# Hashed attention and a feed-forward layer on one core: the first units rearranged, and later heads' maxima half a head closer to their use

## The chip, the cores and the metric

The kernel runs on 1 core of one Trainium2 chip. Times are device microseconds (us). Lower is better. The time before is the median of 3 runs.

## What is computed

```python
# q, k, v: (4, 8, 768, 64); proj: (64, 6); w_in: (512, 2048); w_out: (2048, 512); all float32
q_bucket = sum((q @ proj > 0) * 2**[0..5]);  k_bucket = the same of k
mask = q_bucket[:, None] == k_bucket[None, :]
scores = where(mask, q @ k.T / 8, -1e9)
attn = exp(scores - max(scores)); attn /= attn.sum() + 1e-9
x = (attn @ v), heads side by side: 3072 tokens x 512
h = x @ w_in
g = h if h >= 1, 0 if h <= -1, else (h + 1)**2 / 4
out = g @ w_out
```

There are 32 heads (batch times heads) of 768 queries and keys, taken as 16 pairs of heads.

## The kernel before, in words

**Precision.** Every product is made of three matmuls on float32 values split in a high part and a remainder: high by high, high by low, low by high. Casts make the high parts, subtractions (`sub`, L38, so all of them have line L39 in the profile) the remainders.

**Units.** The attention part works through 384 units. Unit g is head g // 12, one half of its 384 + 384 queries (g % 12 // 6) and one block of 128 keys (g % 6). In this document "unit 6" of a head is the first unit of its second half. A unit makes its scores with two matmuls (L350, L351; `s`), whose operands hold high and low parts and, in eight extra rows, the six hash bits, scaled by 2**36, and the negative row maximum, so that the matmul itself masks and subtracts. ACT takes the exponential twice, once to the rounded high part `ph` (L359) and once in full (L364; `pf` where POOL does the subtraction, otherwise in place). The remainder `pl` is `pf - ph`: on POOL for key blocks 0 and 3, on DVE for the others (`lo_unit`). Four units later (LAG = 4) three matmuls (L383 to L385) add the unit's product with v to an output bank `o`: bank 0 (`obank[0]`) for the first half of the queries, bank 1 for the second. After the last block of a half ACT copies the bank out (L391).

**The maxima.** Before a head's scores can be made, its row maxima of masked products of high parts must be known. For each of its 6 blocks of queries two matmuls (L310, `max_mm`) write to the only `smax` buffer, and DVE reduces it (L314, `max_red`) one unit later. After six such steps, three further steps bring the result into a row: `max_clamp` (L321 and L323, two small operations, on DVE for heads 2 and 3 and on POOL from head 4 on), `max_tr` (L328, a transpose on PE into a bank of `o`) and `max_put` (L333: ACT copies the transpose to `te`, and two DMAs on SP's queue carry it to the row of the operand and to memory).

**Pairs ahead.** While pair p runs, pair p + 2 is prepared: POOL casts the raw q and k (L150) and takes their remainders (L155) in units 0 to 3 of the first (even) head, one cast and one subtraction in each; SP moves parts between partitions (`move`, L161); `bits_mm` (L204, four matmuls) makes the hash bits in unit 7 in bank 1 and in unit 11 in bank 0, each followed by ACT's negative copy (L210) and DVE's comparison (L215); `bits_scale` (L273, POOL) and `bits_put` (L282, four DMAs) store them. The v of pair p + 1 is cast on ACT in unit 6 (L289) and its remainders are taken on POOL in units 7 and 9.

**Order.** Nothing is reordered by a scheduler: each engine's queue holds its instructions in the order in which the program emits them, and an instruction that waits holds up all behind it. In each unit g the loop (L578 to L599) emits: the scores and exponentials of unit g; the reduction of the maxima begun in the unit before; the remainder of unit g - 1; the product with v of unit g - 4; two maxima matmuls if due; and at last the list `tasks[g]`, in the order in which `at` filled it. The splitting of the feed-forward weights, entered first (L1128 and L1140), thus precedes the attention's own tasks of the same unit: in unit 7 of even heads from head 4 on ACT squares a weight tile (L69), in unit 5 it casts one (L87).

**The schedule of the maxima.** Head 0's first three query blocks are reduced by `max_first` ahead of unit 0; a table `early` (L574 to L577) says in which units the maxima of heads 0 to 4 go, up to unit 36; from there on, head h + 2 gets its six steps in units 0, 2, 4, 6, 8, 10 of head h. In terms of the following head, h + 1, the clamp is in its unit 0, the transpose (into bank 1) in its unit 4, the copy in its unit 5 (L543 to L546). Head h + 2 needs the row at its own unit 0.

**The opening.** Pair 0 has no pair ahead of it to hide behind. Lines L436 to L493 load it, make its bits with a faster path (`prep_first`, `place_first`, `first_mm`, `first_cmp`, `first_scale`), reduce its first maxima and write the first half of the row of head 0 by a matmul with the identity (`row_half`, L263). Matmuls on zeros (`keep_busy`, L402) fill pauses. Pair 1's raw data and pair 0's v are loaded in this order (L464, L465), and both heads' remaining steps, with the preparation of pair 1 in quarters (`quarter`), stand in the tasks of units 0 to 15 (L504 to L537).

After the attention comes the feed-forward part (two passes over the weights, PE busy throughout), which the change does not touch.

The statement that sets the place of clamp, transpose and copy:

```python
gc, gt = ((NU + 8, NU + 8), (2 * NU + 4, 2 * NU + 6))[hd] if hd < 2 else (g + NU, g + NU + 4)
at(gc, max_clamp, hd + 2, nc.gpsimd if hd > 1 else nc.vector)
at(gt, max_tr, hd + 2, 1)
at(gt + (hd > 1), max_put, hd + 2)
```

## Time and profile before

| What | Value |
|---|---|
| Median of the runs | 985.98 us (985.34 to 986.76, 3 runs) |
| Profiled execution, its own time | 986.29 us |
| Its span, first to last instruction | 984.5 us |
| Mean granted clock of TensorE | 0.996 |
| HBM | 142 GB/s over the span |

The engines are PE (TensorE's matmuls), PEld (its weight loads, which overlap the matmuls), DVE (VectorE), ACT (ScalarE), POOL (GpSimd) and SP, whose queue issues nearly all DMAs. L12 is line 12 of the kernel. A row of the order of time reads: start, length, engine, line, operation, output <- inputs, shape, number of instructions in it, and in brackets how long the engine had stood idle before it and what ended that. A list of waits reads: who waited, for whom, us in total, times, longest. A row of busy times by stretch gives, for each stretch, its length, each engine's busy time with its number of instructions, the granted clock as a share of full speed, the DMA engines' share and GB/s. The lengths of matmuls overlap: back to back, a matmul of 384 columns is issued every 0.175 us or so, though each row shows 0.34.

### The profile page before, as it was taken

The numbers are of one execution on the slowest core, as the hardware profiler recorded it, in microseconds if no ns is written. First come the engines' busy times: TensorE is split into PE (matmuls) and PEld (weight loads), VectorE is DVE, ScalarE is ACT, GpSimd is POOL, SyncE is SP. The second block draws the span as 40 slices with busy tenths as digits, with TensorE's granted clock in tenths as the row PEclk, the third lists the DMA queues.
The fourth block names the chain that finished last, engine by engine and source line by source line (L and its number), as shares of the span: only waits on it lengthen the run. The fifth ranks groups of instructions, "written<-read, shape, count | busy, mean of one in ns | idle before, by whom it ended". The sixth has DMA issues, their size and how long they took to land.

```text
span 984.5 us, 15564 instructions
## 1 busy us (share of the span) xinstructions
PE 968.2 (98%) x5047; PEld 891.9 (91%) x5047; DVE 799.5 (81%) x1359; ACT 679.3 (69%) x1483; POOL 342.1 (35%) x411
## 2 busy tenths in 40 slices
PE   7999999999999999999999999999999999999998
PEld 5789999999999999999999998888988888988896
DVE  8789999999999999988798887887876777655554
ACT  6779888998999888988655556555564545554444
POOL 7666777778877777766100000000000000000000
PEclk8999999999999999999999999999999999999999
DMA  6654667766656667554496478977449554454431
GB/s 174 177 154 101 174 179 191 199 173 168 177 140 180 173 187 191 136 146 124 127 286 217 118 245 271 299 239 210 118 151 245 147 185 116 130 168 118 115 93 64
DMA packets 94712, 167.55 MB, mean 170 GB/s; under 512 B 13940, under 2 KB 51432, under 8 KB 94632
## 3 DMA queue, kind: packets, MB, share of 16 engines
q1 hardware_dynamic: 94408, 166.56, 59.3%
q8 instruction: 40, 0.66, 0.3%
q14 instruction: 40, 0.33, 0.1%
q10 hardware_dynamic: 224, 0.00, 0.0%
HBM read 106.13 MB, written 33.87 MB: 142 GB/s over the span
## 4 chain that ended last, share of the span: by engine, by line
PE 90%; DVE 5%; ACT 2%; DMA 1%; issue 1%; SPq 0%; DVEq 0%
PE y L791 27%; PE h L1023 18%; PE smax L310 7%; PE h L928 7%; PE o L385 6%; PE s L351 6%; PE o L384 6%; PE o L383 6%; PE s L350 6%; PE o L204 2%; DVE nm L314 2%; DMA vraw<-in_v_dram 1%; DVE pl L39 1%; DMA t<-te 1%; ACT ph L359 0%
## 5 line engine op out<-in xcount | busy, mean ns | idle before, releaser
L359 ACT ACTIVATE ph<-s 128x384 fp32r<-128x384 f32 x380 | 188.1, 495 | 47.5 <-PE s L351 41.8
L314 DVE TENSOR_REDUCE nm<-smax 128x1 f32<-128x768 f32 x189 | 178.9, 947 | 16.2 <-PE smax L310 14.5
L39 POOL TENSOR_TENSOR pl<-pf,ph 128x384 fp32r<-128x384 f32 x128 | 139.0, 1089 | 90.4 <-ACT pf L364 90.1
L756 DVE SCALAR_TENSOR_TENSOR t<-t 128x384 f32<-128x384 f32 x128 | 71.3, 557 | 101.7 <-ACT z L751 101.5
L39 DVE TENSOR_TENSOR pl<-s,ph 128x384 fp32r<-128x384 f32 x256 | 135.5, 544 | 10.2 <-ACT s L364 9.4
L350 PE MATMUL s<-t 128*128 128x384 f32 x384 | 132.6, 345 | 0.0
L385 PE MATMUL o<-pl,va 128*128 128x386 f32 x384 | 130.6, 340 | 0.4 <-DVE pl L39 0.4
L384 PE MATMUL o<-ph,vb 128*128 128x386 f32 x384 | 130.6, 340 | 0.0
L351 PE MATMUL s<-t 128*128 128x384 f32 x384 | 130.3, 339 | 0.2 <-DMA t<-te 0.2
L383 PE MATMUL o<-ph,va 128*128 128x386 f32 x384 | 130.2, 339 | 0.1
L364 ACT ACTIVATE s<-s 128x384 f32<-128x384 f32 x252 | 124.9, 496 | 0.0
L791 PE MATMUL y<-t,ghi 128*128 128x512 f32 x384 | 124.6, 395 | 0.0
L310 PE MATMUL smax<-t 128*128 128x384 f32 x378 | 104.0, 356 | 6.6 <-DVE nm L314 6.1
L750 ACT ACTIVATE t<-h,mh 128x384 f32<-128x384 f32 x56 | 32.6, 581 | 84.4 <-PE h L928 44.3
L310 PEld LDWEIGHTS smax<-t 128*128 128x128 f32 x378 | 65.5, 191 | 23.5 <-DVE nm L314 23.0
L761 ACT CAST ghi<-z 128x384 fp32r<-128x384 f32 x129 | 65.1, 505 | 30.1 <-DVE z L757 26.3
L751 ACT ACTIVATE z<-t,m 128x384 f32<-128x384 f32 x128 | 79.0, 617 | 4.2
L1023 PE MATMUL h<-wbig,t 128*128 128x384 f32 x399 | 81.4, 336 | 0.0
L791 PEld LDWEIGHTS y<-t,ghi 128*128 128x128 f32 x384 | 71.3, 188 | 11.1 <-ACT ghi L761 0.3
L1023 PEld LDWEIGHTS h<-wbig,t 128*128 128x128 f32 x399 | 71.6, 188 | 5.3
L791 PE MATMUL y<-t,glo 128*128 128x512 f32 x192 | 76.0, 396 | 0.0
L791 PE MATMUL y<-woh,glo 128*128 128x512 f32 x192 | 75.7, 394 | 0.2
(181 smaller groups left out, 2092.0 us busy)
## 6 DMA issues: line engine op xcount, KB each, us to landing
t<-wc SPq DMA_DIRECT2D x92, 256.0 KB
t<-t SPq DMA_DIRECT2D x60, 384.0 KB
wraw<-wc SPq DMA_DIRECT2D x76, 256.0 KB
raw<-in_qk_dram SPq DMA_DIRECT2D x15, 768.0 KB
wraw<-in_w_in_dram SPq DMA_DIRECT2D x16, 512.0 KB
wraw<-in_w_out_dram SPq DMA_DIRECT2D x16, 512.0 KB
t<-ed SPq DMA_DIRECT2D x36, 192.0 KB
xd<-xs SPq DMA_DIRECT2D x32, 192.5 KB
```

The costliest lines, as they stand in the source:

```text
L39: eng.tensor_tensor(out=out, in0=a, in1=b, op=ALU.subtract)
L310: nc.tensor.matmul(out=smax[hd][:, hf, 0:HS], lhsT=t2[:, 0, h, i * P:(i + 1) * P], rhs=t2[:, 1, h, hf * HS:(hf + 1) * HS], start=True, sto ...
L314: nc.vector.tensor_reduce(out=nmp(hd)[:, i:i + 1], in_=smax[hd][:, :, 0:HS], axis=AX.XY, op=ALU.max, negate=True)
L350: nc.tensor.matmul(out=ps[:, 0:HS], lhsT=t1[:, 1, h, ks], rhs=t1[:, 0, h, sl], start=True, stop=False)
L351: nc.tensor.matmul(out=ps[:, 0:HS], lhsT=t2[:, 1, h, ks], rhs=t2[:, 0, h, sl], start=False, stop=True)
L359: nc.scalar.activation(out=ph[:, 0:HS], in_=ps[:, 0:HS], func=AF.Exp, scale=SCALE)
L364: nc.scalar.activation(out=pf, in_=ps[:, 0:HS], func=AF.Exp, scale=SCALE)
L383: nc.tensor.matmul(out=o, lhsT=wa, rhs=ph, start=(jj == 0), stop=False)
L384: nc.tensor.matmul(out=o, lhsT=wb, rhs=ph, start=False, stop=False)
L385: nc.tensor.matmul(out=o, lhsT=wa, rhs=pl, start=False, stop=(jj == NJ - 1))
L791: nc.tensor.matmul(out=ys[c][m], lhsT=g_[:, m * P:(m + 1) * P], rhs=w, start=(first and k == 0), stop=(last and k == 2))
L1023: nc.tensor.matmul(out=ps, lhsT=w[:, cs], rhs=x, start=(n == 0 and s not in (2, 3, 6)), stop=(n == 5), skip_group_check=True)
```

## The change

- **v first.** Pair 0's v is loaded ahead of pair 1's raw data, and the latter in two halves of the columns.
- **More on POOL at the start.** The projection's high parts, the cast of pair 0's v, head 1's two scalings (`first_scale`) and the `row_flags` go from ACT and DVE to POOL; the rows of ones and part of the remainders come earlier on POOL's queue.
- **First units.** Head 0's fourth block of maxima goes ahead of unit 0. Head 1's row is written in two halves (units 9 and 14) and not at once (unit 10). Pair 1's quarters go to units 1, 4, 5 and 6, its bits to units 8 and 10, its stores to unit 12; pair 2's casts begin in unit 16 (before: 9), its bits stand in units 20 and 24 (before: 13 and 17). One `move` takes its source from another copy of the same data.
- **Maxima half a head later, for all heads.** The table `early` ends at unit 30; from there on head h + 2 gets its maxima in units 6, 8, 10 of head h and 0, 2, 4 of head h + 1. The clamp is in unit 5 of head h + 1, the transpose in unit 6, the copy in unit 7.

```diff
     def load_raw(pr):
         raws[pr] = work.tile([P, 2, S], F32, name="raw", bufs=1)
-        nc.sync.dma_start(out=raws[pr], in_=qk[pr])
+        for sl in (slice(0, HS), slice(HS, S)) if pr == 1 else (slice(0, S),):
+            nc.sync.dma_start(out=raws[pr][:, :, sl], in_=qk[pr][:, :, sl])
...
-                    (t1[64:128, 0], t1[64:128, 1]), (t2[0:64, 1], t1[64:128, 0]))[part]
+                    (t1[64:128, 0], t1[64:128, 1]), (t2[64:128, 0], t1[64:128, 0]))[part]
...
         if h == 1:
+            ones_row(0)
             for sl in halves:
                 low(sl)
+
+    def ones_row(h):
+        nc.gpsimd.memset(T2[0][32:33, 1, h].bitcast(F32), 1.0)
...
     def row_flags(hd):
-        nc.vector.tensor_scalar(out=nms[hd][:, NJ:2 * NJ], in0=nms[hd][:, 0:NJ], scalar1=CLAMP, scalar2=None,
+        nc.gpsimd.tensor_scalar(out=nms[hd][:, NJ:2 * NJ], in0=nms[hd][:, 0:NJ], scalar1=CLAMP, scalar2=None,
                                 op0=ALU.is_gt)
...
-    def row_half(hd, hf):
-        ps = obank[hf]
+    def row_half(hd, hf, bank=None):
+        ps = ps_m.tile([P, 2, 512], F32, name="smax")[:, 0] if bank is None else obank[bank]
...
+    weights_pair(0)
...
     place_first(0)
+    load_v(0)
     load_raw(1)
-    load_v(0)
...
-    row_half(0, 0)
+    for n in (0, 1):
+        max_mm(0, NJ + n)
+    row_half(0, 0, 0)
+    max_red(0, NJ // 2)
...
+    weights_pair(1)
+    ones_row(1)
+    cast_v(0, nc.gpsimd)
+    split_v(0, nc.gpsimd, 0)
...
-    quarter(0)
-    quarter(1)
-    at(0, first_scale, 1, 1, nc.vector)
-    at(1, cast_v, 0, nc.vector)
...
+    for t in (1, 0):
+        at(0, first_scale, 1, t, nc.gpsimd)
     at(3, row_clamp, 0, NJ // 2, NJ)
+    at(4, row_half, 0, 1, 1)
+    for n, g in enumerate((1, 4, 5, 6)):
+        at(g, quarter, n)
...
+    at(7, row_clamp, 1, 0, NJ // 2)
...
+    at(8, bits_mm, 1, 0, 1)
+    at(9, bits_cmp, 1, 0)
+    at(9, row_half, 1, 0)
+    at(9, row_flags, 0)
+    at(10, bits_mm, 1, 1, 0)
+    at(10, split_v, 0, nc.gpsimd, 1)
...
+    at(14, row_half, 1, 1, 0)
...
         if hd + 2 < NH:
-            gc, gt = ((NU + 8, NU + 8), (2 * NU + 4, 2 * NU + 6))[hd] if hd < 2 else (g + NU, g + NU + 4)
-            at(gc, max_clamp, hd + 2, nc.gpsimd if hd > 1 else nc.vector)
+            gc, gt = (g + NU + 5, g + NU + 6) if hd > 0 else (NU + 8, NU + 8)
+            at(gc, max_clamp, hd + 2, nc.gpsimd if hd > 0 else nc.vector)
             at(gt, max_tr, hd + 2, 1)
-            at(gt + (hd > 1), max_put, hd + 2)
+            at(gt + (hd > 0), max_put, hd + 2)
         if h == 0 and pr + 2 < NPAIR:
-            g0 = g + (9 if pr == 0 else 0)
+            g0 = g + (16 if pr == 0 else 0)
...
-                at(g0 + 7, load_raw, pr + 3)
-            bits_at = ((7, 1), (11, 0)) if pr else ((13, 0), (17, 1))
+                at(g0 + (7 if pr else 4), load_raw, pr + 3)
+            bits_at = ((7, 1), (11, 0)) if pr else ((20, 1), (24, 0))
...
-            at(g + (18 if pr else 21), bits_put, pr + 2)
+            at(g + (18 if pr else 27), bits_put, pr + 2)
...
-            gv = g + LAG + (2 if pr else 10)
+            gv = g + LAG + (2 if pr else 16)
...
-    early = {n: (0, NJ // 2 + n) for n in range(NJ // 2)}
-    for hd, gs in ((1, range(3, 9)), (2, range(14, 20)), (3, (20, 21, 23, 24, 26, 27)),
-                   (4, (28, 29, 31, 32, 34, 35))):
-        early.update({n: (hd, i) for i, n in enumerate(gs)})
+    early = {}
+    for hd, gs in ((0, (0, 2)), (1, (4, 5, 6, 8, 11, 12)), (2, range(14, 20)), (3, (20, 22, 23, 25, 26, 28))):
+        early.update({n: (hd, NJ - len(gs) + i) for i, n in enumerate(gs)})
...
-        if g < 3 * NU:
+        if g < 2 * NU + 6:
...
-            hd, i = g // NU + 2, (g % NU) // 2
+            hd, i = (g - 6) // NU + 2, (g - 6) % NU // 2
```

More of the change, by code (lines that the diff above doesn't have):

```diff
@@ L255, in row_mm @@
                              start=True, stop=True)
-    def row_both(hd):
-        ps = ps_m.tile([P, 2, 512], F32, name="smax")
-        for hf in range(2):
-            row_mm(hd, hf, ps[:, hf])
-        nc.scalar.copy(out=T2[0][32:33, 0, hd, :].rearrange("p (f n) -> p f n", f=2), in_=ps[32:33, :, 0:HS])
-    def row_half(hd, hf):
-        ps = obank[hf]
+    def row_half(hd, hf, bank=None):
+        ps = ps_m.tile([P, 2, 512], F32, name="smax")[:, 0] if bank is None else obank[bank]
         row_mm(hd, hf, ps)
@@ L398, in attention, with keep_busy @@
     scratch = ps_m.tile([P, 2, 512], F32, name="smax")[:, 0]
-    def keep_busy():
-        nc.tensor.matmul(out=scratch[:, 0:2 * P], lhsT=idle[:, 0:P], rhs=idle, start=True, stop=True)
+    def keep_busy(ps=scratch):
+        nc.tensor.matmul(out=ps[:, 0:2 * P], lhsT=idle[:, 0:P], rhs=idle, start=True, stop=True)
     def weights_pair(part):
         if part == 0:
-            nc.scalar.copy(out=pj_hi, in_=pj_raw)
+            nc.gpsimd.tensor_copy(out=pj_hi, in_=pj_raw)
         for i, r, c in ((0, 0, 0), (0, 64, 16), (1, 0, 8), (1, 64, 24)):
@@ L410, in weights_pair @@
             if part == 0:
-                nc.scalar.copy(out=pw[rows, i, c:c + NB], in_=pj_hi[rows].bitcast(F32))
+                nc.gpsimd.tensor_copy(out=pw[rows, i, c:c + NB], in_=pj_hi[rows].bitcast(F32))
             else:
```

47 lines of the change are left out of this document (17 added, 30 removed).

## The prediction

> **What bounds the kernel now.** I read the page first, then the busy time by stage, then the order of time in the first 30 us and in one pair of heads. The page's first lines and its chain:
>
> ```profile
> span 984.5 us, 15564 instructions
> ...
> PE 968.2 (98%) x5047; PEld 891.9 (91%) x5047; DVE 799.5 (81%) x1359; ACT 679.3 (69%) x1483; POOL 342.1 (35%) x411
> ...
> PE 90%; DVE 5%; ACT 2%; DMA 1%; issue 1%; SPq 0%; DVEq 0%
> ```
>
> TensorE (PE) is busy for all but 16 us, and the chain of waits runs over it. So a wait of PE costs its full length, and only PE's waits or PE's work can move the time. The stretches of the attention stage, one line each (the first is head 0 to 3, the second heads 4 to 25, the third the pair of heads 6 and 7; columns: length, busy time of PE, weight loads, DVE, ACT, POOL, then clock and DMA):
>
> ```profile
> 11.80:83.30 71.50, 64.03 (x334) 58.37 (x333) 57.04 (x83) 52.46 (x127) 46.32 (x55) 0.95 0.59 153
> 83.30:389.30 306.00, 305.56 (x1696) 292.25 (x1695) 292.39 (x425) 275.78 (x661) 232.28 (x264) 1.00 0.66 175
> ...
> 110.86:138.73 27.87, 27.84 (x155) 26.57 (x155) 26.75 (x39) 25.11 (x60) 21.04 (x24) 1.00 0.64 175
> ```
>
> Half of PE's idle time, 71.50 - 64.03 = 7.5 us, lies in the first four heads. That is what the rewritten opening can gain from, with some clock besides. Heads 4 to 25 leave 0.4 us idle in 306: nothing is to be gained there, but a wait put into each pair of heads counts some twelve times. So the change has a place to win about once and a place to lose repeatedly, and I cost both.
>
> **The opening, units 0 to 6.** In order of time:
>
> ```profile
> 5.53 0.73 POOL L468 MEMSET t<- 1x768 f32 x1 [2.52 <-DVE t L39]
> ...
> 10.02 0.29 POOL L493 MEMSET pl<- 128x2 f32 x7
> ...
> 11.84 0.34 PE L350 MATMUL s<-t 128*128 128x384 f32 x1
> ...
> 15.29 0.56 DVE L289 CAST va<-vraw 128x768 fp32r<-128x768 f32 x1 [1.48 <-DMA vraw<-in_v_dram]
> ...
> 16.76 0.30 PEld L310 LDWEIGHTS smax<-t 128*128 128x128 f32 x2 [2.26 <-DVE nm L314]
> ...
> 17.09 0.99 DVE L241 TENSOR_SCALAR t<-xs,cvd 8x768 fp32r<-8x768 f32 x1
> ...
> 17.63 2.27 POOL L39 TENSOR_TENSOR vb<-vraw,va 128x384 fp32r<-128x384 f32 x2
> ...
> 18.01 0.94 DVE L314 TENSOR_REDUCE nm<-smax 128x1 f32<-128x768 f32 x1
> ...
> 20.82 0.99 POOL L39 TENSOR_TENSOR pw<-pj_raw,pj_hi 64x6 fp32r<-64x6 f32 x4
> ```
>
> And from the PE's own list, and POOL's of a later head:
>
> ```profile
> 26.80 0.34 PE L350 MATMUL s<-t 128*128 128x384 f32 x1
> ```
>
> ```profile
> 129.34 1.42 POOL L273 TENSOR_SCALAR bits<-neg,cvt 32x768 fp32r<-32x768 f32 x1
> ```
>
> Unit 0 begins at 11.84 and unit 7 at 26.80: 14.96 us for seven units. DVE waits 1.48 us for v (`vraw`), everything behind it on its queue waits too, and PE waits 2.26 us for DVE's reduction. The clock then falls:
>
> ```profile
> 14.75:18.16 3.41, 1.06 (x5) 1.00 0.48 125
> 18.16:21.58 3.42, 2.58 (x8) 0.50 0.41 88
> 21.58:24.99 3.41, 3.41 (x14) 0.50 0.85 202
> ```
>
> In the stretch before the fall PE is busy for 1.06 of 3.41 us; the next two run at a granted 0.50. With v first and its cast, plus head 1's two scalings, on POOL, DVE keeps only reductions, subtractions and comparisons. Unit 0 should still begin near 11.84, since what leads up to it (the reductions of head 0's first key blocks, then the row) is unchanged. POOL becomes the next late one. Its memsets end at 10.3 (10.02 + 0.29), about 9.8 with the row of ones of 5.53 moved behind its first casts; then come the four projection remainders (0.99), the second row of ones (0.73), the cast of v (two of POOL's casts of 0.50, quoted with head 6), one remainder of v (1.1, half of 2.27) and the two scalings. A scaling took DVE 0.99; for POOL the nearest row is that of `bits`, 1.42, so 2.8 for two. The sum ends at 16.4. Head 1's first maximum (unit 4) waits for it, and three maxima with a reduction of 0.94 us each follow, in units 4, 5 and 6; unit 7 would begin near 20. That gains 6.8 us, the two half-clock stretches included.
>
> Part of it is work put off. The bits of pair 1 (four matmuls, 0.7 us) and one unit's maxima (0.35) come later: -1.05. The schedule behind it adds waits: in unit 20 the clamp, transpose, copy and bits of head 2 all stand in one unit; in units 30 and 31 POOL has two pairs' casts behind it and head 3's clamp last. I put 1 us to the first, 2.3 to the others, and take 0.7 off for row copies that are now halves: 2.6. The opening is worth -6.8 + 1.05 + 2.6 = **-3.2 us**; bounds -9 (no new wait, and the rest of the idle goes) and +3 (the casts of pair 3 wait for their late load).
>
> **The pairs of heads from 4 on.** The edit that runs through the kernel moves a head's clamp (L321, L323) from unit 0 to unit 5, its transpose (L328) from unit 4 to 6 and the copy of the transpose (`te`, L333) from unit 5 to 7. Head 6, which begins at 111.20, by engine. POOL, the order of time without the other engines:
>
> ```profile
> 112.28 0.23 POOL L321 TENSOR_SCALAR nm<-nm 128x6 f32<-128x6 f32 x1 [1.50 <-DVE nm L314]
> 112.59 0.23 POOL L323 TENSOR_SCALAR nm<-nm 128x6 f32<-128x6 f32 x1
> 112.77 0.50 POOL L150 CAST t<-raw 128x384 fp32r<-128x384 f32 x1
> 113.36 1.02 POOL L39 TENSOR_TENSOR t<-raw,t 128x384 fp32r<-128x384 f32 x1
> 114.34 1.47 POOL L39 TENSOR_TENSOR pl<-pf,ph 128x384 fp32r<-128x384 f32 x1
> ...
> 120.86 2.18 POOL L39 TENSOR_TENSOR pl<-pf,ph 128x384 fp32r<-128x384 f32 x2
> ```
>
> ACT:
>
> ```profile
> 112.13 0.48 ACT L364 ACTIVATE pf<-s 128x384 f32<-128x384 f32 x1
> ...
> 117.56 0.49 ACT L359 ACTIVATE ph<-s 128x384 fp32r<-128x384 f32 x1
> ...
> 118.87 0.25 ACT L333 CAST te<-o 12x128 fp32r<-12x128 f32 x1
> ...
> 119.78 0.82 ACT L289 CAST va<-vraw 128x768 fp32r<-128x768 f32 x1
> 120.51 0.48 ACT L359 ACTIVATE ph<-s 128x384 fp32r<-128x384 f32 x1
> 120.89 0.47 ACT L364 ACTIVATE s<-s 128x384 f32<-128x384 f32 x1
> 121.30 0.66 ACT L69 ACTIVATE wsq<-wraw 128x512 f32<-128x512 f32 x1
> ```
>
> PE, where unit 7 begins at 119.27:
>
> ```profile
> 116.91 0.27 PE L328 MATMUL o<-ident,nm 128*12 128x128 f32 x1
> ...
> 118.82 0.62 PE L310 MATMUL smax<-t 128*128 128x384 f32 x2
> ...
> 119.27 0.34 PE L350 MATMUL s<-t 128*128 128x384 f32 x1
> ...
> 120.15 0.87 PE L204 MATMUL o<-t,pw 128*128 128x384 f32 x4
> ...
> 123.96 0.30 PEld L310 LDWEIGHTS smax<-t 128*128 128x128 f32 x2 [0.26 <-DVE nm L314]
> ```
>
> First wait, PE for POOL. Today the clamp is ahead of the four casts and four subtractions that POOL does for a later pair in units 0 to 3; in unit 5 it stands behind them and behind the `pl` of key blocks 0 and 3. POOL is free at 110.78 (1.50 before 112.28), and its first cast and subtraction (112.77 to 114.34) would be over at 112.4. The `pl` then needs `pf`, ready at 112.61. From that `pl` at 114.34 to the end of key block 3's (the first of the two from 120.86, 121.95) the trace has 7.6 us without a pause, so the clamp would start at 120.25 and end 0.54 later (112.28 to 112.82), at 120.8. If none of those operations is stretched (a cast 0.50, a subtraction 1.02), the 7.6 is about 6.8 and the clamp ends at 120.0. PE is at the transpose by 119.1, behind the maxima of 118.82: it waits 0.9 to 1.7 us, with all its queue (units 7 and on) behind it. Nothing covers this.
>
> Second wait, PE for ACT. The copy of the transpose must be done before bank 1 takes the bits of unit 7 (L204). Today the copy comes two units ahead; now both stand in unit 7, the copy behind that unit's two exponentials and the square of a weight (L69). That this order stalls PE is in the trace once, in head 1, where copy and next use of a bank are adjacent (list of waits of the first 70 us):
>
> ```profile
> PEld o L383 <- ACT te L333: 0.4, 1, 0.4
> ```
>
> With the transpose at 120.8, unit 7's exponential starts 0.65 later, as 117.56 stands to 116.91: 121.45. Exponentials 0.85, square 0.60, copy 0.25: 123.15. The bits start at 123.2 in place of 120.15, **3.05 us** later, both waits together. Lower bound: with no first wait ACT is free of the v cast at 120.4 and the same three steps end at 122.1, +2.0. Upper bound: another stretched POOL operation of 0.5, +3.5. DVE catches up meanwhile, so the 0.26 at 123.96 goes, about 0.2: net 2.85. I take this value, since the rows without gaps are the ones that repeat.
>
> How often: POOL's clamp waits in the same way in 12 heads (list of waits, 80 to 480 us).
>
> ```profile
> POOL nm L321 <- DVE nm L314: 16.6, 12, 1.5
> ```
>
> These are the even heads 4 to 26, the ones with casts and bits. 12 x 2.85 = **+34.2 us** (bounds 22 and 40).
>
> Odd heads have no casts and no bits in bank 1 at that place. Their clamp follows the last reduction by one unit and POOL is free, so PE waits only for the clamp's own 0.54, less the maxima in between: 0.1 in each of 14 heads, **+1.4** (0 to 5, if the row's transfer, now issued behind the four of the bits on SP's queue, lands late for the next head).
>
> Sum against the profiled execution's own 986.29 us (its span 984.5 and 1.8 around it; the median of three is 985.98): 986.3 - 3.2 + 34.2 + 1.4 = **1018.7, so 1019 us**. The other edits (flags to POOL, second head's row in halves, another source for one move, memsets reordered) lie beside these waits in the first two heads and are in the opening's bounds. Three maxima move past the end of head 29, to where PE has room: nothing.
>
> **The rivals.** *The clock falls too.* Between 119.1 and 123.2 PE would be busy for about 0.95 us only, less than the 1.06 of 3.41 that preceded the fall at 18.16. If the stretch that is judged is a fixed 3.41 us long, it lies inside those 4.1 us in one case of five, and in one of two if some more work is allowed. Two stretches at 0.50 cost up to 3.4 us, as they did there, about 2.8 with the rest of the wait in them. Four of twelve heads: +11, 1030 us (1026 to 1037). The Trainium skill, "TensorE: Matmul & The Clock Gate" (Part 1), has a free-running window of 3413 ns and half rate after an idle window; taken by the word, a window with 0.95 us of work is not idle and the clock stays, 1019. The row at 14.75 speaks against that reading: 31% busy, and the clock halved.
>
> *Only one of the waits.* If POOL's work ends in time, or ACT's copy finds a gap, 1.3 us stay per head: 986.3 - 3.2 + 15.6 + 1.4 = 1000. For it: POOL begins up to 2 us earlier than now. Against: both waits are chains without a pause.
>
> *Faster.* The opening's 6.8 us come in full and the clamp's place costs nothing: if clamp and copy were done by 119.1 and 120.15, PE would never stand. The time is 986.3 - 3.2 - 1, 982. It decides at 0.2 us per even head, where the opening's gain is used up. Against it: the 7.6 us of POOL work cannot begin before `pf`, at 112.6.
>
> **How the numbers follow.** Two waits, clock kept: 0.43. Clock falling in some heads: 0.27. One wait: 0.17. Faster: 0.06. The last 0.07 are smaller waits (below 0.8 us per head) against the opening's gain: 0.05 of it slower, 0.02 within the bound of no change. A measurement of this kernel can tell about 0.2% (2 us). Slower 0.92, same 0.02, faster 0.06. The range, 1001 to 1037, holds the forecast's bounds and reaches into both neighbours.
>
> **What would show it.** In the list of waits: PE at L328 for POOL's clamp, about 1.5 us in 12 heads or more, and PE at L204 for the copy of L333, about 1.3 us in as many; a pair of heads 31 us long in place of 27.87; unit 7 beginning near 20 us with the clock at 1.00 to there. The prediction is wrong if a pair of heads still takes 27.9 us, if the bits of unit 7 start without a wait, or if unit 7 of head 0 begins after 24.

## The result, and the profile after

The kernel after takes 1049.79 us (median of 4 runs, 1048.7 to 1052.36), the kernel before beside it 985.66 (4 runs, 984.81 to 986.76): ratio 1.0654, 95% interval 1.0631 to 1.0677. The forecast was 1019 with a range to 1037. The profiled execution has a time of 1052.36 us. Its page:

```profile
span 1050.6 us, 15602 instructions
...
PE 992.9 (95%) x5047; PEld 914.7 (87%) x5047; DVE 786.8 (75%) x1352; ACT 684.3 (65%) x1479; POOL 348.6 (33%) x424
...
PE 74%; POOL 11%; ACT 5%; issue 3%; DMA 3%; DVE 3%; SPq 0%; POOLq 0%; ACTq 0%; DVEq 0%
```

TensorE runs as many matmuls as before (x5047), yet is idle for 58 us instead of 16, and POOL now holds 11% of the chain on which it did not appear. The three stretches, cut at the same units as before (heads 0 to 3, heads 4 to 25, the pair of heads 6 and 7; columns: length, busy time of PE, weight loads, DVE, ACT, POOL, then clock and DMA):

```profile
13.10:91.59 78.49, 65.71 (x327) 58.12 (x325) 47.81 (x73) 51.89 (x123) 47.94 (x58) 0.91 0.54 138
91.59:450.75 359.16, 325.54 (x1696) 313.00 (x1695) 285.31 (x425) 280.08 (x661) 233.58 (x265) 0.92 0.56 150
125.28:157.22 31.94, 28.69 (x156) 27.95 (x156) 25.75 (x39) 25.41 (x61) 21.39 (x25) 0.95 0.57 153
```

This pair took 27.87 us and takes 31.94, with 3.25 us of idle PE and a clock below 1; the twelve pairs from head 4 on take 30.5 to 33.7. By the starts of the units the 66.1 us of longer span divide like this:

| Stretch | Before | After | Difference | Forecast |
|---|---|---|---|---|
| span's start to unit 0 | 11.84 | 13.10 | +1.3 | 0 |
| units 0 to 6 | 14.96 | 7.70 | -7.3 | -6.8 |
| units 7 to 47 | 56.51 | 70.79 | +14.3 | +3.65 |
| units 48 to 335 (heads 4 to 27) | 334.07 | 389.67 | +55.6 | +35.6 |
| units 336 to 381 | 46.68 | 48.80 | +2.1 | 0 |
| the rest | 520.4 | 520.5 | +0.1 | 0 |

**The pairs of heads.** The list of waits from 90 to 480 us (total, times, longest), those of PE and of its weight loads:

```profile
PEld o L327 <- POOL nm L322: 28.6, 17, 2.4
...
PE o L327 <- POOL nm L322: 23.1, 12, 2.1
PEld o L209 <- ACT te L332: 17.2, 12, 1.5
PE o L209 <- ACT te L332: 12.8, 12, 1.2
```

These are the two waits of the forecast, in the twelve even heads (L327 was L328 before, L332 was L333, L209 was L204). The rows of PEld and PE cover the same gaps and are not added. In head 6, which begins at 125.28, POOL, ACT and PE read:

```profile
133.38 1.01 POOL L39 TENSOR_TENSOR pl<-pf,ph 128x384 fp32r<-128x384 f32 x1
134.34 0.42 POOL L320 TENSOR_SCALAR nm<-nm 128x6 f32<-128x6 f32 x1
134.84 0.23 POOL L322 TENSOR_SCALAR nm<-nm 128x6 f32<-128x6 f32 x1
```

```profile
136.58 0.66 ACT L69 ACTIVATE wsq<-wraw 128x512 f32<-128x512 f32 x1
137.14 0.24 ACT L332 CAST te<-o 12x128 fp32r<-12x128 f32 x1
```

```profile
132.50 0.52 PE L309 MATMUL smax<-t 128*128 128x384 f32 x2
135.12 0.28 PE L327 MATMUL o<-ident,nm 128*12 128x128 f32 x1 [2.10 <-POOL nm L322]
...
137.43 1.65 PE L209 MATMUL o<-t,pw 128*128 128x384 f32 x4 [1.15 <-ACT te L332]
```

PE stops at the transpose until POOL's clamp ends at 135.07, and again at the bits, whose bank the copy frees at 137.38. The bits start 137.43 - 125.28 = 12.15 us into the head, against 120.15 - 111.20 = 8.95 before: 3.20 later (forecast 3.05), and 2.97 to 3.60 later in the twelve. But these four matmuls then take 1.65 us, not 0.87: the clock has fallen. PE's busy time and clock in stretches of 3.41 us, head 6, head 10 and head 18:

```profile
133.43:136.85 3.42, 1.16 (x6) 1.00 0.98 226
136.85:140.26 3.41, 2.83 (x9) 0.50 0.64 139
198.29:201.70 3.41, 1.72 (x8) 1.00 0.86 196
328.00:331.40 3.40, 1.95 (x11) 1.00 0.84 175
331.40:334.81 3.41, 2.27 (x14) 1.00 0.96 231
```

Ten of the twelve even heads (all but 18 and 26) have one or two stretches at 0.50; from unit 48 to unit 336 they add up to 54.6 us.

**The opening.** Units 0 to 6 take what was forecast. Of the 14.3 us behind them 9.3 lie in units 30 and 31, 3.4 in unit 24 and 1.75 in unit 20. POOL, SP's queue and PE, in order of time:

```profile
57.87 0.51 POOL L151 CAST t<-raw 128x384 fp32r<-128x384 f32 x1 [7.99 <-DMA raw<-in_qk_dram]
...
63.51 0.97 POOL L272 TENSOR_SCALAR bits<-neg,cvt 32x768 fp32r<-32x768 f32 x1
```

```profile
50.02 0.38 SPq L146 DMA_DIRECT2D raw<-in_qk_dram  x1
50.44 8.69 SPq L162 DMA_DIRECT2D t<-t  x2
...
64.51 2.78 SPq L281 DMA_DIRECT2D t<-bits  x4
```

```profile
51.53 0.69 PE L350 MATMUL s<-t 128*128 128x384 f32 x1 [2.00 <-DMA t<-te]
...
67.72 0.98 PE L309 MATMUL smax<-t 128*128 128x384 f32 x2 [6.25 <-DMA t<-bits]
```

The raw pair 3 is issued at 50.02, in unit 24, whose task is its first cast. POOL waits 7.99 us for it; pair 2's bits stand behind that cast and are sent from 64.51 on. The first maxima of head 4, in unit 30, need them: 6.25 us of idle PE, and 10.2 us of half clock from 65.2. In unit 24 PE waits 2.00 us for the row of head 2, and 3.4 us at half clock follow. SP stands too: its row at 50.44 holds two moves of pair 2, and in 7.6 of its 8.69 us the second waits until a move has landed; the first stands behind that load.

### The profile page after: what moved, and what is told of

Read it like the earlier page. It is cut to its first block, busy times and chain, and to the rows that moved or that the text cites. A ratio compares the mean times of both kernels' runs of the same rounds, so it can differ in the third digit from the quotient of the medians.

```text
span 1050.6 us, 15602 instructions
## 1 busy us (share of the span) xinstructions
PE 992.9 (95%) x5047; PEld 914.7 (87%) x5047; DVE 786.8 (75%) x1352; ACT 684.3 (65%) x1479; POOL 348.6 (33%) x424
## 4 chain that ended last, share of the span: by engine, by line
PE 74%; POOL 11%; ACT 5%; issue 3%; DMA 3%; DVE 3%; SPq 0%; POOLq 0%; ACTq 0%; DVEq 0%
PE y L793 25%; PE h L1025 17%; PE h L930 6%; POOL t L39 4%; PE smax L309 4%; PE s L350 4%; PE s L349 4%; PE o L383 4%; PE o L384 4%; PE o L382 4%; POOL pl L39 3%; PE o L209 3%; POOL t L151 2%; ACT ph L358 1%; ACT s L363 1%
## 5 line engine op out<-in xcount | busy, mean ns | idle before, releaser
L39 POOL TENSOR_TENSOR pl<-pf,ph 128x384 fp32r<-128x384 f32 x128 | 143.0, 1117 | 148.5 <-ACT pf L363 142.9
L349 PE MATMUL s<-t 128*128 128x384 f32 x384 | 136.7, 356 | 0.0
L350 PE MATMUL s<-t 128*128 128x384 f32 x384 | 134.0, 349 | 2.0 <-DMA t<-te 2.0
L384 PE MATMUL o<-pl,va 128*128 128x386 f32 x384 | 133.8, 348 | 0.7 <-DVE pl L39 0.4
L383 PE MATMUL o<-ph,vb 128*128 128x386 f32 x384 | 133.9, 349 | 0.0
L382 PE MATMUL o<-ph,va 128*128 128x386 f32 x384 | 133.4, 347 | 0.0
L309 PEld LDWEIGHTS smax<-t 128*128 128x128 f32 x378 | 69.9, 196 | 18.8 <-DVE nm L313 10.6
L350 PEld LDWEIGHTS s<-t 128*128 128x128 f32 x384 | 76.0, 198 | 2.4 <-DMA t<-te 2.3
L384 PEld LDWEIGHTS o<-pl,va 128*128 128x128 f32 x384 | 75.4, 196 | 1.8 <-DVE pl L39 1.8
L349 PEld LDWEIGHTS s<-t 128*128 128x128 f32 x384 | 75.9, 198 | 1.1
```

Of the source, the lines that this page charges most:

```text
L39: eng.tensor_tensor(out=out, in0=a, in1=b, op=ALU.subtract)
L309: nc.tensor.matmul(out=smax[hd][:, hf, 0:HS], lhsT=t2[:, 0, h, i * P:(i + 1) * P], rhs=t2[:, 1, h, hf * HS:(hf + 1) * HS], start=True, sto ...
L349: nc.tensor.matmul(out=ps[:, 0:HS], lhsT=t1[:, 1, h, ks], rhs=t1[:, 0, h, sl], start=True, stop=False)
L350: nc.tensor.matmul(out=ps[:, 0:HS], lhsT=t2[:, 1, h, ks], rhs=t2[:, 0, h, sl], start=False, stop=True)
L382: nc.tensor.matmul(out=o, lhsT=wa, rhs=ph, start=(jj == 0), stop=False)
L383: nc.tensor.matmul(out=o, lhsT=wb, rhs=ph, start=False, stop=False)
```

## Experiments

Theory A: the two waits of the even heads, the clock that falls around them, and in the opening the order on POOL and SP are the whole loss. Rivals: the late maxima cost by themselves, or transfers limit the opening. All the runs (unit 48 and units 48 to 335 by the profiled execution), each against the kernel before on the same chip:

| Run | us | Ratio (95%) | Unit 48 at | Units 48 to 335 |
|---|---|---|---|---|
| before | 985.66 | 1 | 83.31 | 334.1 |
| after | 1049.79 | 1.0654 (1.0631 to 1.0677) | 91.59 | 389.7 |
| e1_late_only | 1040.91 | 1.0569 (1.0547 to 1.0591) | 80.23 | 388.8 |
| e2_opening_only | 992.80 | 1.0071 (1.0054 to 1.0087) | 90.70 | 333.8 |
| e3_filled_wait | 1031.32 | 1.0466 (1.0450 to 1.0481) | 87.90 | 372.2 |
| e4_bits_later | 1029.65 | 1.0447 (1.0432 to 1.0463) | 87.49 | 370.5 |
| e7_no_waits | 1013.76 | 1.0275 (1.0258 to 1.0292) | 88.59 | 352.4 |
| e8_opening_fixed | 1046.12 | 1.0610 (1.0591 to 1.0629) | 87.78 | 390.8 |
| e9_all | 1012.54 | 1.0260 (1.0245 to 1.0275) | 86.58 | 353.7 |
| e10_late_no_waits | 1004.76 | 1.0189 (1.0172 to 1.0205) | 79.77 | 352.2 |
| e11_two_units_later | 1048.18 | 1.0629 (1.0611 to 1.0647) | 79.71 | 397.8 |
| e12_after_later | 1056.96 | 1.0720 (1.0700 to 1.0741) | 87.82 | 396.8 |
| e13_later_reordered | 1057.11 | 1.0724 (1.0707 to 1.0741) | 86.86 | 396.4 |
| e14_unit7 | 1019.66 | 1.0336 (1.0320 to 1.0353) | 80.07 | 368.6 |
| e15_unit7_opening | 1026.02 | 1.0404 (1.0377 to 1.0431) | 86.43 | 368.8 |
| e16_before_order | 994.02 | 1.0084 (1.0070 to 1.0098) | 79.88 | 342.4 |
| e17_raw_behind | 1007.17 | 1.0228 (1.0202 to 1.0254) | 80.52 | 354.3 |
| e18_one_cast_act | 988.27 | 1.0028 (1.0016 to 1.0039) | 79.45 | 337.6 |
| e19_two_casts_act | 988.99 | 1.0037 (1.0024 to 1.0051) | 81.13 | 337.5 |

### The two halves of the change, each alone

e1 has the late schedule in the kernel before, e2 the opening of the kernel after with the schedule of before. The edit of e1 (in which head 4 goes from `early` too):

```diff
-            gc, gt = (...)[hd] if hd < 2 else (g + NU, g + NU + 4)
+            gc, gt = (...)[hd] if hd < 2 else (g + NU + 5, g + NU + 6)
-        if g < 3 * NU:
+        if g < 2 * NU + 6:
-            hd, i = g // NU + 2, (g % NU) // 2
+            hd, i = (g - 6) // NU + 2, (g - 6) % NU // 2
```

> The opening of the kernel before, with only the later maxima, clamps, transposes and copies of the change. Theory A (the loss sits in the pairs of heads from 4 on: PE waits for POOL's clamp in unit 6 and for ACT's copy in unit 7 of even heads, and the clock halves after them): units 48 to 336 take 389 us as in the changed kernel and not 334, the time is 986 + 55 = 1041 us, 1033 to 1050. Rival B (the rearranged opening upsets the transfers and the order for the rest of the run): below 1000 us. Rival C (half and half): 1010 to 1025.

> The changed opening up to unit 29, head 4's maxima caught up in units 30 to 35, then the schedule of the kernel before. Theory A: unit 48 comes 8 to 11 us late (the waits of units 24, 30 and 31 stay, the catching up costs 2 to 3 us), each later pair takes 27.9 us again: 994 to 999 us. Rival B: pairs still take over 30 us, 1030 us or more.

Both came out near theory A: 1040.91, and 992.80, 1.2 us below its band. The late schedule makes nearly all of the loss: units 48 to 335 take 388.8 us with it and 333.8 without. In the opening of before it even helps: unit 48 starts at 80.23, 3.1 us earlier. Of these, 0.8 us lie ahead of unit 7, where both kernels issue the same, so they are not the schedule's. Units 7 to 47 take 2.3 us less; three blocks of maxima, six matmuls or 1.0 us, only move behind unit 48, and the shorter units are 28, 29 and 35, in which `early` places no maxima any more. The new opening alone costs 7.4 us at unit 48.

### What the clock costs, and the second wait alone

In e3 twelve matmuls of zeros stand ahead of the transpose of each even head from 4 on, so that PE is busy where it waited. In e4 the bits go one unit later.

```diff
+            if hd % 2 and 2 < hd < 26:
+                for _ in range(12):
+                    at(gt, keep_busy, obank[1])
             at(gt, max_tr, hd + 2, 1)
```

```diff
-            bits_at = ((7, 1), (11, 0)) if pr else ((20, 1), (24, 0))
+            bits_at = ((8, 1), (11, 0)) if pr else ((20, 1), (24, 0))
```

> The changed kernel with twelve matmuls of 256 columns on zeros ahead of the transpose in unit 6 of the even heads 4 to 26, about 1.7 us of PE work that nobody reads. Theory A (PE waits 2.1 us there anyway, and the clock halves because PE is busy for less than about half of a 3.41 us stretch): the work costs nothing, the clock stays at 1.00 in heads 4 to 26, a pair takes 30.3 us in place of 32.5: 1050 - 25 = 1025 us, 1020 to 1034. Rival (the clock falls for another reason, or the wait is not there): 1050 us or up to 1070.

> The changed kernel with the first half of the bits of pairs 3 to 15 one unit later (unit 8 and not 7), so that ACT's copy of the transpose has a unit to finish. Theory A: PE at the bits no longer waits for the copy (1.2 to 1.5 us in 12 heads, 17 us), the wait for POOL of 2.1 us stays, and the clock falls in fewer heads or for one stretch only (5 to 15 us less): 1018 to 1030 us. Rival (ACT itself is late, the wait only moves by a unit): 1045 to 1052 us.

Waits of PE in e3, then in e4, 92 to 480 us:

```profile
PE o L209 <- ACT te L332: 13.7, 12, 1.2
PE o L327 <- POOL nm L322: 6.0, 9, 0.7
```

```profile
PE o L327 <- POOL nm L322: 23.0, 12, 2.1
PE o L382 <- DVE neg L220: 8.7, 12, 1.0
```

Both times lie in theory A's bands. In e3 the second wait is the same as in the kernel after (13.7 against 12.8) and the filling only takes the place of the first, yet units 48 to 335 take 17.5 us less, with one stretch of 3.4 us at half clock. So the clock cost at least about 17 us there; half of the 54.6 us at half clock, 27.3, is the most. In e4 the second wait is gone, the first is as long as ever, and from head 6 on the clock stays at 1.00. PE's busy time and clock around the wait in head 4, then in head 6:

```profile
94.43:97.84 3.41, 1.35 (x9) 1.00 0.74 159
97.84:101.25 3.41, 3.41 (x13) 0.50 0.87 210
125.15:128.56 3.41, 1.99 (x12) 1.00 0.55 120
```

In head 4 the whole wait of 2.06 us lies in one stretch, and the clock falls; in the other heads an edge of the stretches cuts it. They stay cut because a pair here takes about 30.7 us, nine stretches. So a wait of 2 us alone can bring the clock down, and that it did so once in twelve is partly luck. The waits of e4 are 4 us shorter in sum than those of the kernel after, units 48 to 335 take 19 us less; most of the gain is therefore clock. Its price is a new wait: the output matmuls of unit 10 take the bits' bank, and DVE's comparison now ends too late for them.

### Both waits removed, and the opening reordered

e7 changes the kernel after so that DVE makes the clamps and the copy stands in the transpose's unit. e8 changes the opening's order alone. e9 is both. e10 has e7's two edits in e1.

```diff
-            at(gc, max_clamp, hd + 2, nc.gpsimd if hd > 0 else nc.vector)
+            at(gc, max_clamp, hd + 2, nc.gpsimd if hd == 1 else nc.vector)
-            at(gt + (hd > 0), max_put, hd + 2)
+            at(gt, max_put, hd + 2)
```

```diff
-            g0 = g + (16 if pr == 0 else 0)
+            g0 = g + (16 if pr == 0 else 3 if pr == 1 else 0)
...
-            at(g0 + 3, move, pr + 2, 0)
-            at(g0 + 3, move, pr + 2, 1)
+            for n in (0, 1):
+                at(g0 + (3 if pr else 5), move, pr + 2, n)
...
-            bits_at = ((7, 1), (11, 0)) if pr else ((20, 1), (24, 0))
+            bits_at = ((7 + (pr == 1), 1), (11, 0)) if pr else ((20, 1), (24, 0))
```

> The kernel after with two lines of the schedule changed: the clamps of all later heads stay on DVE (as the tail of the work that they wait for), and the copy of the transposed maxima stands in the transpose's own unit, ahead of the exponentials of the next unit and of the cast of the values. Both waits of the even heads should go. Theory A (the two waits of unit 6 and 7, and the clock that falls in the stretch around them, are the whole loss of the steady part): units 48 to 336 take 324 to 336 us instead of 389.7, the clock stays at 1.00 there, and since the opening keeps its 8 us the time is 985 to 997. Rival B (the late maxima cost by themselves, by what they push on DVE or PE): units 48 to 336 stay above 350 us and the time above 1008.

> The kernel after with the opening's order alone changed: the casts of pair 3 begin three units later, behind the scaling of pair 2's bits on POOL, and the moves of pair 2 stand behind the row of head 2 on SP's queue; the steady part is left as it is. Theory A (POOL's cast for pair 3 waits for its load, and pair 2's bits stand behind it): the wait of about 6 us of the first maxima of head 4 goes, and with it the half clock around unit 30; unit 48 starts at 77 to 84 us instead of 91.6, and the time is 1034 to 1043. Rival B (the first units run into a limit of transfers, so that the wait returns elsewhere in the opening): unit 48 stays after 87 us and the time at 1045 to 1052.

> The two edits together: clamps on DVE and copy in the transpose's unit, and the opening's order with pair 3's casts three units later. Theory A, by which the losses lie apart and add up: unit 48 at 77 to 84 us, units 48 to 336 in 324 to 336 us, the time 972 to 986, so faster than the kernel before by up to 1.4%. Rival B (either repair fails): 990 or more.

> The opening of before with the late maxima, the clamps on DVE and the copy in the transpose's unit. Theory A: unit 48 at 80 us as in the run of the late maxima alone, units 48 to 336 in 324 to 336 us, the time 975 to 988. It tells whether the late maxima are themselves a gain once nothing waits for them: if units 48 to 336 take under 332 they are, at 334 they are neutral, above 340 they cost.

Theory A missed in all four: e7, e9 and e10 lie 17 to 27 us above the upper end of their bands, e8 3. The bands of rival B hold in e7, e8 and e9; the rows below show the causes. In e7 the bits wait no more and the clock stays, but the transpose waits for DVE. The waits and the clamp's durations (ns, min/median/max):

```profile
PE o L327 <- DVE nm L322: 15.6, 16, 1.1
```

```profile
L322 DVE TENSOR_SCALAR nm<-nm x27: 171/911/941, 96.7 to 476.1; 128x6 f32<-128x6 f32 x27
```

The same 128x6 operation takes 0.17 us or 0.91. Two of them, in head 8 and in head 11:

```profile
156.44 0.23 DVE L320 TENSOR_SCALAR nm<-nm 128x6 f32<-128x6 f32 x1
156.61 1.95 POOL L39 TENSOR_TENSOR pl<-pf,ph 128x384 fp32r<-128x384 f32 x2
...
156.70 0.92 DVE L322 TENSOR_SCALAR nm<-nm 128x6 f32<-128x6 f32 x1
```

```profile
201.83 0.17 DVE L322 TENSOR_SCALAR nm<-nm 128x6 f32<-128x6 f32 x1
```

Of the 27, 15 take 0.91 to 0.94 us; in each an operation of POOL began about 0.1 us earlier, and the clamp ends 0.02 to 0.04 us behind it (here the first of the two, at 157.59). The other 12 meet no POOL operation and take 0.17. The Trainium skill, "SBUF — State Buffer" (SBUF: two separate sides), says that GpSimd, and VectorE in a mode that uses two ports or with two inputs in SBUF, take a shared pair of ports as an exclusive lock for a whole instruction. These 27 rows agree with such a lock; which mode the clamp runs in, no row here shows. So DVE is no way round POOL: where the two meet, it waits for POOL's operation all the same.

In e8 the opening's wait stays 6.4 us long, for another reason than the one removed. SP's queue:

```profile
47.18 11.34 SPq L162 DMA_DIRECT2D t<-t  x4
...
61.14 2.78 SPq L281 DMA_DIRECT2D t<-bits  x4
```

```profile
SPq L162 <- DMA t<-t: 8.0, 1, 8.0
```

Pair 2's four moves, issued behind the load of pair 3, hold SP for 11.34 us, 8.0 of them while the last waits until one ahead of it has landed, and the bits come behind them. The kernel after has the same wait beside POOL's (7.6 us), so with POOL's alone removed the bits still come late.

e10 shows the late maxima with the old opening: unit 48 at 79.77, but 18 us lost in units 48 to 335, 15.3 of them in waits of the transpose for DVE.

### Transpose and row two units later

e11 is e1 with the transpose, copy and row in unit 8 and the bits' halves at units 11 and 13 in the other bank. e12 is the same in the kernel after; e13 also puts pair 2's bits ahead of its last move and of the load of pair 3, and pair 3's casts ten units later.

```diff
-            gc, gt = (...)[hd] if hd < 2 else (g + NU + 5, g + NU + 6)
+            gc, gt = (...)[hd] if hd < 2 else (g + NU + 5, g + NU + 8)
-            at(gt + (hd > 1), max_put, hd + 2)
+            at(gt, max_put, hd + 2)
...
-            bits_at = ((7, 1), (11, 0)) if pr else ((13, 0), (17, 1))
+            bits_at = ((11, 0), (13, 0)) if pr else ((13, 0), (17, 1))
```

And e13 beyond e12 (old line, then new; pair 2's first moves and pair 3's bits change their places too):

```diff
-            g0 = g + (16 if pr == 0 else 0)
+            g0 = g + (16 if pr == 0 else 10 if pr == 1 else 0)
...
-                at(g0 + (7 if pr else 4), load_raw, pr + 3)
+                at(g0 + (7 if pr else 12), load_raw, pr + 3)
...
-            at(g + n + 1, move, pr + 2, 3)
+            at(g + n + (1 if pr else 4), move, pr + 2, 3)
...
-            at(g + (18 if pr else 27), bits_put, pr + 2)
+            at(g + (21 if pr == 1 else 18 if pr else 26), bits_put, pr + 2)
```

> The opening of before and the late maxima, with the clamps on POOL as in the kernel after, but transpose and copy together in unit 8 instead of units 6 and 7, and both halves of the bits in bank 0, at units 11 and 13. Theory A (the late maxima cost only because their transpose stands less than 2.4 us behind the last score of unit 6, which DVE and POOL cannot make): no wait is left at the transpose or at the bits, units 48 to 336 take 322 to 332 us against 334 of the kernel before, and the time is 974 to 985. Rival B (the row then comes too late): the first scores of each head wait 0.5 us or more for the row's transfer, units 48 to 336 take 336 us or more and the time is 988 or more.

> The kernel after with the same steady schedule (transpose and copy in unit 8, bits at units 11 and 13 in bank 0) and its opening as it is. Theory A: units 48 to 336 in 322 to 332 us, unit 48 still at 87 to 92 us because of the opening's waits, the time 982 to 994. Rival B as for the run before: 996 or more.

> The run before with the opening's transfers in another order: pair 2's moves behind the row of head 2, its bits ahead of its last move and of the load of pair 3, and the casts of pair 3 ten units later. Theory A (the wait for the bits at unit 30 is the order on SP and POOL alone): the wait goes, unit 48 starts at 76 to 83 us, the time is 970 to 984. Rival B (the transfers of the opening are bound by bandwidth, so that the wait moves to another transfer): unit 48 stays at 85 or later and the time at 982 or more.

Rival B's bands hold in all three, and the time is about that of the kernel after or worse. Waits and SP's queue in e11:

```profile
PE s L351 <- DMA t<-te: 38.3, 12, 4.1
```

```profile
158.36 1.22 SPq L145 DMA_DIRECT2D raw<-in_qk_dram  x1
...
162.34 0.76 SPq L335 DMA_DIRECT2D t<-te  x1
```

No wait is left at the transpose or the bits. The row, whose copy ended at 159.38, is now issued at 162.34 behind the load of the next raw pair and lands at 166.06, and the next head's scores wait up to 4.1 us for it; the clock falls again in nine heads. So a late row is bounded on both sides: by POOL's clamp, and by what SP issues from unit 7 on. In e13 the wait at unit 30 is gone (units 30 to 33 take 1.23, 0.90, 1.26 and 0.96 us), and unit 36 starts at 67.17 in place of 78.83: that part of the opening's loss was order, on SP and POOL, not a limit of the transfers as rival B has it. From unit 36 to 48 a wait of 2.7 us for a late row of this schedule, and the half clock around it, take 6.9 us back.

### The window between

e14 is e1 with transpose, copy and row in unit 7, the moves and the next load behind them (units 7, 8 and 9), the last quarter's cast and subtraction behind the clamp (unit 6), bits at units 11 and 13, sent in unit 20. e15 is that with e13's opening, pair 3's casts twelve units later. e16 undoes in e14 the new places of moves, raw loads and casts. e17 is e14 with the next raw pair at unit 14 and the values at unit 20.

```diff
-            gc, gt = (...)[hd] if hd < 2 else (g + NU + 5, g + NU + 6)
+            gc, gt = (...)[hd] if hd < 2 else (g + NU + 5, g + NU + 7)
...
-            at(g + (18 if pr else 21), bits_put, pr + 2)
+            at(g + (20 if pr else 21), bits_put, pr + 2)
```

These lines are in e14 and e16. In e14 alone (e17 has 14 for the 9 of the load, and `gv + 14` for the values; e15 has the same three lines for the pairs from 4 on):

```diff
-                at(g0 + n, cast_h, pr + 2, nc.gpsimd, n % 2, n // 2)
+                gn = g0 + (6 if n == 3 and pr else n)
+                at(gn, cast_h, pr + 2, nc.gpsimd, n % 2, n // 2)
...
-            at(g0 + 3, move, pr + 2, 0)
-            at(g0 + 3, move, pr + 2, 1)
-            at(g0 + 6, move, pr + 2, 2)
+            for n in range(3):
+                at(g0 + ((7, 7, 8) if pr else (3, 3, 6))[n], move, pr + 2, n)
...
-                at(g0 + 7, load_raw, pr + 3)
+                at(g0 + (9 if pr else 7), load_raw, pr + 3)
```

> The opening of before and the late maxima; transpose, copy and the row's transfer together in unit 7, with the moves and the load of the next raw pair behind the row on SP's queue (units 7, 8 and 9), the last quarter's cast and low part on POOL behind the clamp (unit 6), the bits in bank 0 at units 11 and 13 and their four transfers at unit 20. Theory A (the late row has a window between POOL's and DVE's clamp, 2.4 us after unit 6 begins, and the transfers that SP issues from unit 7 on, and the window can be opened by moving the neighbours): no wait over 0.4 us at the transpose, none at the bits, none of a score for its row; units 48 to 336 in 324 to 334 us, the time 974 to 987. Rival B (no room: the row's transfer stays late behind the moves): a wait of over 0.5 us per pair of heads for the row, the time 990 or more.

> The same steady schedule behind the opening of after, with pair 2's bits ahead of its last move and of the load of pair 3 on SP, and pair 3's casts twelve units later. Theory A (the opening's 8 us are three waits behind each other on SP and POOL): unit 48 at 77 to 81 us, the time 971 to 985. Rival B: a transfer of the opening stays late, unit 48 at 84 or later, the time 982 or more.

> The opening of before and the late maxima, with transpose, copy and the row's transfer in unit 7 ahead of the load of the next raw pair, the bits in bank 0 at units 11 and 13 and their transfers at unit 20; moves, casts and loads stand where they stood before. Theory A (the weights' transfer, for which ScalarE's square waited 2.9 us ahead of the copy in the odd heads of the run before, came late only because the raw pair was issued ahead of it): no wait for that transfer; at the transpose of the even heads 0.3 to 0.6 us for POOL's clamp are left; units 48 to 336 in 326 to 338 us, the time 976 to 990. Rival B (the transfers of a pair of heads fill the queue in any order that puts the row late): a wait of over 1 us per pair for a transfer, 995 or more.

> The run with everything in unit 7, with the load of the next raw pair at unit 14 instead of 9 and that of the values at unit 20 instead of 12, so that both stand behind the weights' transfer on SP's queue. Theory A: the wait of ScalarE's square for the weights goes, no wait over 0.4 us is left in even or odd heads, units 48 to 336 in 324 to 334 us, the time 973 to 986. Rival B: the row of the odd heads then comes behind the raw pair and the first scores wait for it by 0.5 to 1.5 us per pair; the time 986 to 1005.

e14 lies 33 us above theory A's band, e15 41. In e14 no wait is left at the transpose or the bits, but in the odd heads a transfer is late. Waits of PE, and ACT in head 9:

```profile
PE o L383 <- ACT te L333: 19.9, 11, 2.9
```

```profile
168.79 0.68 ACT L69 ACTIVATE wsq<-wraw 128x512 f32<-128x512 f32 x1 [2.95 <-DMA wraw<-in_w_in_dram]
169.36 0.24 ACT L333 CAST te<-o 12x128 fp32r<-12x128 f32 x1
```

A weight of the later stage now comes behind the raw pair; ACT's square waits 2.95 us for it, the copy stands behind the square, and PE behind the copy. e16 gives the transfers their old order and this wait is gone, as theory A had it; the time, 994.02, is 4 us above its band, mostly because the transpose still waits for POOL:

```profile
PE o L328 <- POOL nm L323: 5.8, 8, 0.7
```

e17 fell out by rival B's cause, 2 us above its band: the odd heads' rows wait behind the raw pair (21.8 us in 11 heads). e15 has e14's loss and an opening that reaches unit 36 at 66.43, level with e14's 66.59; up to unit 48 it then loses 6.5 us to e14: PE waits 2.1 us at the bits for POOL's casts and subtractions, and the clock is at half for 6.8 us.

### The last wait

e18 and e19 are e16 with one and two of the four casts of each later pair on ACT instead of POOL, ahead of the clamp.

```diff
+                if pr and n in (3,):
+                    at(g0 + n, cast_act, pr + 2, n % 2, n // 2)
+                else:
+                    at(g0 + n, cast_h, pr + 2, nc.gpsimd, n % 2, n // 2)
```

> The run in the transfer order of before, with the cast of the last quarter of each later pair on ScalarE instead of POOL. Theory A (what is left of that run's loss in the even heads, 0.9 us at the transpose, is POOL's clamp standing behind four casts and low parts): POOL reaches the clamp 0.5 to 1.0 us earlier, the wait falls to 0.0 to 0.4 us in each of 9 heads, and the time is 984 to 990. Rival B (ScalarE then is late with the exponentials): the wait moves to the scores, 994 or more.

> As the run before, with the casts of the last two quarters on ScalarE. Theory A: the transpose waits no more, 980 to 988, level with the kernel before or a little below. Rival B as for the run before: 992 or more.

e18 is in its band (988.27), e19 a little above (988.99). The wait of the transpose falls to 0.6 us in one head; no other is over 1.5 us in total. The stretch of units 48 to 335 in e18:

```profile
79.45:417.06 337.61, 334.17 (x1850) 318.45 (x1850) 324.71 (x465) 302.58 (x732) 242.19 (x276) 1.00 0.62 170
```

PE is busy for all but 3.4 us, and the stretch still takes 337.6 us against 334.1 before, where PE was idle for 0.7. So the late maxima, with nearly every wait removed, end 0.28% (0.16 to 0.39) behind the kernel before: they bring nothing here, and heads 4 to 27 had only 0.7 us of idle time to give back. No version of these runs is faster than the kernel before.

## Why the prediction was right and wrong

**Direction and the two waits: right.** Slower was given 0.92. The bits of head 6 start 3.20 us later (3.05 forecast), those of all twelve even heads about as much, for POOL's clamp and ACT's copy as named. The split differs: 2.10 and 1.15 us in head 6, where 1.5 and 1.3 were to be seen. With the clock kept, in e3, units 48 to 335 take 38.1 us more than before, near the forecast's 35.6.

**The clock: the step that failed.** It failed in "Two waits, clock kept: 0.43", on which the forecast of 1019 stands, and in the rival's four of twelve heads. The one row of before (1.06 of 3.41 us busy, then a fall) was taken for the limit, with "some more work" as an afterthought. The clock fell in ten of twelve heads, after stretches with up to 1.72 us of work, and stayed in the two with 1.93 and 1.95. With a limit near half a stretch, a gap of 4 us with 0.95 us of work nearly always leaves one stretch below it; heads 18 and 26 kept the clock because an edge cut their gap in half. The rival's +11 was 17 to 27 us. That is most of the 55.6 - 35.6 = 20.0 us that the steady part took above the forecast. The prediction's other reading, that a window with some work is not idle and the clock stays, failed with it: 1.16 us of work did not save the clock.

**The opening: the sign failed.** Its first half was right: units 0 to 6 take 7.3 us less (6.8 forecast), unit 7 begins at 20.80 (near 20), the clock stays 1.00. "Unit 0 should still begin near 11.84" was 1.3 us off; 0.6 of it are DVE's step ahead of the row, which took 0.17 us before and now ends 0.02 us behind POOL's second row of ones, moved beside it:

```profile
11.55 0.76 DVE L250 TENSOR_SCALAR nrow<-nm 128x3 fp32r<-128x3 f32 x1
```

```profile
11.56 0.73 POOL L190 MEMSET t<- 1x768 f32 x1
```

The failed step is "I put 1 us to the first, 2.3 to the others": units 7 to 47 took 14.3 us more, not 3.65. Unit 20, the first, took 1.75 more, units 30 and 31, the others, 9.3; the 3.4 of unit 24 were not foreseen. The load of pair 3 coming too late for POOL's casts was named, but as the bound of +3; priced by its row it is 7.99 us of POOL with pair 2's bits behind it, a wait on SP of nearly the same length beside it, then half clock. e2, with the new opening and none of the late schedule behind it, shows 7.4 us of loss at unit 48. e13 shows that the wait at unit 30 goes with the order on SP and POOL; that the whole opening could come out ahead was not shown.

**Small terms.** The odd heads' +1.4 did not come: in five of the twelve from 5 to 27 the transpose waits 0.34 us for the clamp, yet the twelve together take 155.6 us against 156.7 before. So the steady loss lies whole in the even heads. "Three maxima move past the end of head 29 ... nothing" was +2.1 us between units 336 and 382; 1.0 of it are the six matmuls of 0.17 us, for head 29, that moved behind unit 336. In the trace another 0.35 lies at the transpose of unit 366, and 0.9 in units 370 and 371, where the last product waits for DVE's remainder; why DVE ends later there was not tried. The rivals of one wait and of a faster kernel fell in the kernel after itself; e16 and e18 show what it takes to remove the waits, and that there is no gain behind them.

## What to carry to other kernels

Where the busiest engine has no idle time in a stretch, bringing a dependent step closer to its use has nothing to win there and can cost: first ask what the slack was covering (here POOL's backlog, ACT's order, SP's queue and the transfers, one behind the other). When a wait on TensorE is forecast, ask at once how much work stands in the 3.4 us around it, since two short waits close together, or one of 2 us that lies whole in one stretch, brought the clock down here, which cost half as much again as the waits. In an opening, follow each load to the first instruction that needs it, and then to what stands behind that instruction on its engine.

## What the runs showed of the hardware

The granted clock changes on a fixed grid of 3.413 us (all edges of the kernel after lie on it). In the even heads it fell after each stretch with 1.15 to 1.72 us of PE work and did not after 1.93 and 1.95. The limit is not sharp: in the traces of all the runs 89 of 90 falls come after 1.76 us or less, one after 2.00, and 14 stretches with 1.58 to 1.81 us did not bring it down. In the kernel after it came back after one stretch with 2.83 us or more (once, at 2.88, it did not), and after 2.33 to 2.65 it took another one. The Trainium skill, "TensorE: Matmul & The Clock Gate" (Part 1), gives the window of 3413 ns, with which the grid agrees, and half rate after at least one idle window, with which the falls after 1.15 to 1.72 us of work do not agree.

DVE's 128x6 clamp took 0.17 us alone and 0.91 to 0.94 while POOL ran a subtraction. A tiny instruction on DVE can take as long as the POOL operation beside it.
